# Attention and two expert layers on one core: another order of the steps up to the third block of the first experts

## The chip, the cores and the metric

The kernel runs on one core of a Trainium2 chip. The metric is the device time of one execution in microseconds (us); lower is better. The engines are called by the profile's names: PE is TensorE (PEld its weight loads), DVE is VectorE, ACT is ScalarE, POOL is GpSimd, SP is the engine whose queue issues every DMA of this kernel.

## The reference

A gated linear attention over 768 time steps (2 batches, 8 heads of 40) is followed by two expert layers on 1536 tokens of width 320. All inputs are 64-bit floats.

```python
m_new = np.maximum(f_gate[:, :, t] + m, i_gate[:, :, t])
f_stab = np.exp(f_gate[:, :, t] + m - m_new)
i_stab = np.exp(i_gate[:, :, t] - m_new)
C = f_stab * C + i_stab * np.einsum('bhd,bhe->bhde', vt, kt)
n = f_stab * n + i_stab * kt
y[:, :, t] = sigmoid(o_gate) * (C @ qt) / np.maximum(np.abs(n . qt), 1.0)
...
x = (x @ w_a) * (x @ w_b) @ w_out          # first experts, 320 -> 1536 -> 320
h = x @ w_in                               # second experts, 320 -> 2048 -> 320
x = np.maximum(0.01 * h, h) @ w_out
```

## The kernel before

The time axis is cut into six pieces `p` of 128 steps, for each of the two batches `b`. A piece of attention goes through these steps (the names are those in the table `ORDER`, the lines those of the profile): `dsc` (L351) scans the forget gates into a 128x128 decay for four heads on DVE; `smm` (L373) forms the scores on PE; `sat` (L378) multiplies both on DVE; `out` (L422) forms the outputs on PE; `onm` (L433 to L435), `og` (L440, POOL), `nrm` (L481) and `nd` (L486, ACT) divide by the norm and apply the output gate; `xmm` (L493) transposes the result, and `xh` (L507, ACT) and `xl` (L513, DVE) split it into a rounded part and a rest. `stm` (L448) and `ste` (L468) form the state that the next piece starts from; `gist` (L323, L324) transposes the input gates.

Ahead of the first piece stand the gates: `lg` loads them (the first 128 steps as `lg:0`, the other 640 as `lg:1`), `gs` (L274) scans them, `gfa`, `gfb`, `gi` (L281, L285, L289) take differences, `gef` and `gei` (L292) take exponentials on ACT, `gfr` (L295 to L297) rounds the first 128, `gdec` (L300, L301) and `gcum` (L309) prepare the other pieces, `dmm` (L341) spreads the first piece's gates over the partitions, and `idr` (L699) copies four identities for the scans.

The weights arrive as 64-bit floats in tiles of 128 x 768 (or 640) words. `lw` (L209) loads one: 128 x 768 x 8 bytes are 0.786 MB. `dh` (L224) and `dl` (L228) decode its two halves on ACT, `dm` (L232) joins them on DVE, `dr` (L241, L251) rounds on ACT, `ds` (L246, L247, L256) forms the rest on POOL. `up` (L562) multiplies a block of tokens with one pair of weight tiles: it takes four passes over `xh` first, then passes over `xl`, for each of two halves. The blocks 0 and 1 of the first experts have 256 tokens (one piece of both batches), the third, block 2, has 512. `e1`, `em`, `eh`, `el` work on the product, and `dn` (L620 to L622) multiplies it with the second weight matrix.

`spin` (L329) is a matmul over a tile of zeros, 512 columns wide, into a PSUM tile that nobody reads.

The order is written out by hand: `ORDER` lists all 1116 steps, and the last loop of the kernel issues them one after the other. So each engine works off its own instructions in the order of the table, and waits at an instruction until what that one needs is there. A load on SP also waits for the load eight places ahead of it, and for the buffer that it fills.

Of the kernel before, what the change touches and what calls it, by code (L numbers as in the profile page):

```python
# [37 lines left out]
    dm:2 onm:0:1 dm:4 out:0:0 lc:1 lf:1:0 lw:3 scum dr:4 og:0:1 smm:1:0 dsc:1:0:1 onm:0:0 dh:3 dr:2 dsc:1:0:0
    og:0:0 lw:6 lk:1:0 lq:1:0 ld:1:0 stm:0:0 stm:0:1 ds:4 sat:1:0:0 nrm:0:1 nrm:0:0 lf:1:1 sat:1:0:1 dl:3
    ste:0:1 nd:0:0 ds:2 val:1:0 ste:0:0 nd:0:1 vo:1:0 xmm:0:0 xmm:0:1 xh:0:0 lk:1:1 lw:5 ls:1:1 lw:7 lq:1:1  # L40
    ld:1:1 xh:0:1 xl:0:0 xl:0:1 up:0:1 up:0:0 dm:3 dl:6 dh:6 qry:1:0 dr:3 e1:0:1 e1:0:0 dm:6 em:0:1 em:0:0
    sig:1:0 eh:0:0 eh:0:1 out:1:0 ds:3 el:0:1 onm:1:0 el:0:0 dsc:1:1:1 up:0:3 dr:6 dh:5 sig:1:1 dl:5 val:1:1
    og:1:0 ds:6 vo:1:1 qry:1:1 dm:5 up:0:2 lw:8 e1:0:3 nrm:1:0 em:0:3 dsc:1:1:0 e1:0:2 dn:0:0 smm:1:1 dh:7 dl:7
    dr:5 nd:1:0 sat:1:1:0 sat:1:1:1 em:0:2 dm:7 lk:2:0 lq:2:0 lw:9 eh:0:2 up:0:4 lf:2:0 dl:8 dr:7 eh:0:3 out:1:1
    xmm:1:0 dh:8 key:1:0 ds:5 onm:1:1 dn:0:1 el:0:2 el:0:3 dn:0:2 og:1:1 xh:1:0 e1:0:4 nrm:1:1 xl:1:0 em:0:4
    dm:8 ds:7 dn:0:3 nd:1:1 stm:1:0 xmm:1:1 eh:0:4 dl:9 xh:1:1 up:0:5 dr:8 xl:1:1 ste:1:0 ds:8 e1:0:5 up:1:0
    em:0:5 el:0:4 lw:10 ls:2:0 lk:2:1 vo:2:1 val:2:0 key:1:1 up:1:1 smm:2:0 dh:9 eh:0:5 e1:1:0 dsc:2:0:0 dm:9
    em:1:0 el:0:5 dh:10 dl:10 eh:1:0 e1:1:1 dr:9 sat:2:0:0 dsc:2:0:1 sat:2:0:1 el:1:0 em:1:1 lq:2:1 lw:12 lw:11
    ld:2:0 ls:2:1 stk:1:0 key:2:0 dn:0:4 up:1:3 dn:0:5 stm:1:1 dn:1:0 eh:1:1 e1:1:3 dl:12 el:1:1 dm:10 em:1:3
    dn:1:1 up:1:2 up:1:4 dr:10 dh:11 eh:1:3 e1:1:2 em:1:2 vo:2:0 ds:9 qry:2:0 ds:10 el:1:3 sig:2:1 e1:1:4 eh:1:2  # L50
    stm:2:0 up:1:5 ste:1:1 em:1:4 el:1:2 dh:12 eh:1:4 e1:1:5 up:0:6 lf:2:1 lw:13 lf:3:0 ld:2:1 ls:3:0 lw:15
    dm:12 el:1:4 dl:11 e1:0:6 dsc:2:1:0 em:1:5 ls:4:0 em:0:6 lk:3:1 dsc:2:1:1 dm:11 dn:1:2 dn:1:3 up:0:7 dn:1:4
    out:2:0 eh:1:5 dh:13 dr:11 eh:0:6 dr:12 sig:2:0 el:1:5 dsc:3:0:1 e1:0:7 up:1:6 onm:2:0 em:0:7 key:2:1
    ste:2:0 el:0:6 e1:1:6 eh:0:7 dl:13 ds:12 ds:11 val:2:1 og:2:0 up:1:7 dn:0:6 dn:1:5 el:0:7 em:1:6 nrm:2:0
    dm:13 smm:2:1 qry:2:1 stk:1:1 lw:14 lw:16 lf:3:1 up:0:8 dl:15 e1:1:7 eh:1:6 dr:13 sat:2:1:0 dl:14 dh:14
    el:1:6 stk:2:0 ds:13 dl:16 nd:2:0 em:1:7 sat:2:1:1 eh:1:7 dh:15 e1:0:8 dsc:3:1:0 dn:1:6 out:2:1 dn:0:7
    up:0:9 em:0:8 el:1:7 dm:14 dn:1:7 dm:15 stm:2:1 onm:2:1 dsc:3:1:1 dr:14 up:1:8 e1:0:9 eh:0:8 dr:15 og:2:1
    val:3:1 ds:14 em:0:9 ste:2:1 nrm:2:1 nd:2:1 dh:16 eh:0:9 el:0:8 e1:1:8 xmm:2:1 xmm:2:0 up:1:9 dn:0:8 el:0:9
    ld:3:1 lk:3:0 lw:17 em:1:8 ds:15 vo:3:0 lq:3:0 ls:3:1 lk:4:0 lf:4:0 lq:3:1 dm:16 eh:1:8 e1:1:9 xh:2:0 xh:2:1
    xl:2:0 em:1:9 dsc:3:0:0 eh:1:9 ld:3:0 dr:16 sig:3:0 xl:2:1 stk:2:1 ds:16 vo:3:1 el:1:8 dn:0:9 up:0:10  # L60
    up:1:10 val:4:0 val:3:0 qry:3:0 dn:1:8 smm:3:0 e1:0:10 dl:17 sig:3:1 dh:17 el:1:9 em:0:10 e1:1:10 eh:0:10
    sat:3:0:0 el:0:10 sat:3:0:1 dm:17 dr:17 dn:1:9 up:0:11 key:3:1 em:1:10 out:3:0 eh:1:10 e1:0:11 el:1:10
    onm:3:0 em:0:11 up:1:11 eh:0:11 e1:1:11 og:3:0 ds:17 key:3:0 vo:4:0 qry:3:1 nrm:3:0 smm:3:1 el:0:11 dn:0:10
    sat:3:1:0 em:1:11 dn:0:11 stm:3:0 sat:3:1:1 eh:1:11 nd:3:0 out:3:1 ste:3:0 el:1:11 onm:3:1 xmm:3:0 dn:1:10
    dn:1:11 lq:4:0 xh:3:0 ls:5:1 og:3:1 nrm:3:1 xl:3:0 nd:3:1 xmm:3:1 stk:3:0 xh:3:1 ye:0 xl:3:1 stm:3:1 up:2:0
    dsc:4:0:0 ste:3:1 e1:2:0 em:2:0 lk:5:1 ld:4:0 smm:4:0 dsc:4:0:1 key:4:0 qry:4:0 up:2:1 sat:4:0:1 sat:4:0:0
    eh:2:0 e1:2:1 ye:1 lf:5:1 ls:4:1 lf:4:1 ld:4:1 lk:4:1 stm:4:0 out:4:0 em:2:1 el:2:0 dsc:4:1:1 eh:2:1 sig:4:0
    onm:4:0 dsc:5:1:0 lq:4:1 dn:2:0 up:2:2 e1:2:2 el:2:1 em:2:2 vo:5:1 og:4:0 up:2:3 dn:2:1 eh:2:2 sig:4:1
    e1:2:3 ste:4:0 nrm:4:0 el:2:2 em:2:3 dsc:4:1:0 lk:5:0 lf:5:0 lq:5:0 ld:5:0 ls:5:0 smm:4:1 dn:2:2 up:2:4
    eh:2:3 e1:2:4 sat:4:1:1 sig:5:1 em:2:4 el:2:3 up:2:5 stk:3:1 val:5:0 qry:5:0 key:4:1 val:4:1 val:5:1 qry:4:1  # L70
    eh:2:4 e1:2:5 sat:4:1:0 dsc:5:0:1 em:2:5 el:2:4 vo:4:1 nd:4:0 stk:4:0 up:2:6 xmm:4:0 dn:2:3 out:4:1 dn:2:4
    eh:2:5 e1:2:6 em:2:6 el:2:5 xh:4:0 eh:2:6 up:2:7 e1:2:7 el:2:6 onm:4:1 og:4:1 dsc:5:0:0 nrm:4:1 nd:4:1
    xl:4:0 em:2:7 stm:4:1 xmm:4:1 up:2:8 eh:2:7 sig:5:0 xh:4:1 e1:2:8 dn:2:5 dsc:5:1:1 em:2:8 el:2:7 ste:4:1
    xl:4:1 lq:5:1 ld:5:1 up:2:9 smm:5:0 e1:2:9 eh:2:8 sat:5:0:1 em:2:9 sat:5:0:0 el:2:8 up:2:10 smm:5:1 dn:2:6
    qry:5:1 stk:4:1 vo:5:0 sat:5:1:0 sat:5:1:1 e1:2:10 eh:2:9 out:5:1 dn:2:7 out:5:0 em:2:10 onm:5:0 onm:5:1
    og:5:0 og:5:1 up:2:11 el:2:9 nrm:5:0 nrm:5:1 e1:2:11 nd:5:1 nd:5:0 xmm:5:1 xmm:5:0 xh:5:0 eh:2:10 xh:5:1
    dn:2:8 em:2:11 el:2:10 xl:5:0 xl:5:1 ca lw:19 lw:20 dn:2:9 up:4:0 e1:4:0 dh:19 eh:2:11 lw:21 em:4:0 el:2:11
    up:4:1 dn:2:10 dn:2:11 dh:20 eh:4:0 dl:19 dl:20 e1:4:1 dm:20 el:4:0 em:4:1 dm:19 eh:4:1 dr:19 up:4:2 e1:4:2
    dh:21 dr:20 ye:2 dl:21 ds:19 ds:20 lw:25 lw:18 em:4:2 el:4:1 up:4:3 dn:4:0 ym:0:1 ym:0:0 eh:4:2 lw:22 yh:0:1
    yh:0:0 e1:4:3 em:4:3 yl:0:0 el:4:2 dn:4:1 dm:21 up:4:4 dh:22 dl:22 dr:21 e1:4:4 eh:4:3 dl:18 dh:25 dh:18  # L80
    yl:0:1 ym:0:2 em:4:4 el:4:3 dn:4:2 ds:21 up:4:5 yh:0:2 dl:25 e1:4:5 eh:4:4 em:4:5 lw:26 dm:18 dm:25 el:4:4
    dn:4:3 ym:0:3 up:4:6 dm:22 dh:26 dr:25 eh:4:5 dr:22 dl:26 e1:4:6 yl:0:2 dm:26 el:4:5 em:4:6 dn:4:4 dr:18
# [721 lines left out]
```

## Time and profile before

| | before |
|---|---|
| time, median of 3 runs | 449.29 us (448.03 to 450.08) |
| the profiled execution's own time | 449.11 us |
| its span, first to last instruction | 447.3 us |
| PE busy | 434.6 us (97%) |
| DVE, ACT, POOL busy | 210.6, 208.6, 126.3 us |
| HBM read | 44.1 MB |

The span is cut into 40 slices on the profile's page, and one digit gives the busy tenths of a slice. Waits are listed with the engine and line that waited and what ended the wait. The timeline lists instructions by start, with the idle time of the engine ahead of them in square brackets. The granted clock of TensorE is 1.00 at 2.4 GHz and 0.50 at 1.2 GHz.

### The profile page before, as it was taken

How to read it: one execution, taken by the hardware profiler on the slowest of the kernel's cores; microseconds unless marked ns; L12 is line 12 of the kernel's file. 1: busy time of each engine (PE TensorE's matmuls, PEld its weight loads, DVE VectorE, ACT ScalarE, POOL GpSimd, SP SyncE). 2: the span in 40 equal slices, each digit the busy share in tenths (PEclk: the TensorE clock that was granted, in tenths of full speed). 3: DMA queues.
4: the chain of work that ended last, by engine and by line, in shares of the span. 5: the costliest groups of instructions: out<-in, count | busy, mean ns of one | idle time of the engine just before them, and what ended most of it. 6: DMA issues, size and time to landing. Idle time of an engine off the chain costs nothing.

```text
span 447.3 us, 8216 instructions
## 1 busy us (share of the span) xinstructions
PE 434.6 (97%) x3350; PEld 391.2 (87%) x3350; DVE 210.6 (47%) x352; ACT 208.6 (47%) x381; POOL 126.3 (28%) x135
## 2 busy tenths in 40 slices
PE   6789999999999999999999999999999999999996
...
PEclk9559999999999999999999999999999999999999
...
GB/s 247 292 320 284 301 235 268 231 211 55 141 170 94 61 34 1 1 186 106 134 59 139 110 171 77 8 52 0 1 59 1 1 1 1 1 59 1 0 1 59
DMA packets 25799, 46.69 MB, mean 104 GB/s; under 512 B 1885, under 2 KB 18849, under 8 KB 25761
## 3 DMA queue, kind: packets, MB, share of 16 engines
...
q8 instruction: 26, 0.43, 0.4%
q14 instruction: 12, 0.10, 0.1%
...
## 4 chain that ended last, share of the span: by engine, by line
PE 91%; DVE 4%; ACT 1%; issue 1%; POOL 1%; DMA 1%; SPq 0%; DVEq 0%; ACTq 0%
PE mm L562 29%; PE mm L589 20%; PE dn L620 11%; PE dn L622 11%; PE dn L621 11%; PE pa L373 2%; PE pa L422 1%; DVE pp L351 1%; PE pa L415 1%; PE pa L493 1%; PE pa L448 1%; DVE y L232 1%; PE pa L652 1%; DMA ident_all<-consts 1%; PE mm L448 1%
## 5 line engine op out<-in xcount | busy, mean ns | idle before, releaser
L562 PE MATMUL mm<-xh,wa 128*128 128x256 f32 (+1 forms) x480 | 116.4, 343 | 0.6 <-ACT xh L507 0.6
L562 PEld LDWEIGHTS mm<-xh,wa 128*128 128x128 f32 x480 | 80.9, 192 | 10.2 <-ACT xh L507 1.0
L605 DVE TENSOR_TENSOR gl<-gg,gh 128x512 fp32r<-128x512 f32 x48 | 34.2, 730 | 99.4 <-ACT gh L600 95.3
L562 PE MATMUL mm<-xl,wa 128*128 128x256 f32 (+1 forms) x288 | 79.9, 339 | 0.0
L595 ACT ACTIVATE gg<-mm 128x512 f32<-128x512 f32 x48 | 28.1, 595 | 72.3 <-PE mm L589 70.9
L620 PE MATMUL dn<-wa,gh 128*128 128x320 f32 x192 | 59.5, 310 | 0.0
L622 PE MATMUL dn<-wa,gl 128*128 128x320 f32 x192 | 59.3, 309 | 0.0
L621 PE MATMUL dn<-wa,gh 128*128 128x320 f32 x192 | 59.2, 309 | 0.0
L562 PEld LDWEIGHTS mm<-xl,wa 128*128 128x128 f32 x288 | 51.9, 192 | 5.8
L572 DVE TENSOR_TENSOR gg<-gg,mm 128x256 f32<-128x256 f32 (+1 forms) x48 | 26.2, 546 | 59.4 <-PE mm L562 35.3
L567 ACT ACTIVATE gg<-mm 128x256 f32<-128x256 f32 (+1 forms) x48 | 23.4, 488 | 61.9 <-PE mm L562 43.8
L620 PE MATMUL dn<-wd,gh 128*128 128x320 f32 x144 | 46.0, 319 | 0.0
L622 PE MATMUL dn<-wd,gl 128*128 128x320 f32 x144 | 44.6, 310 | 0.4 <-DVE gl L581 0.4
L621 PE MATMUL dn<-wd,gh 128*128 128x320 f32 x144 | 44.4, 308 | 0.0
L581 DVE TENSOR_TENSOR gl<-gg,gh 128x256 fp32r<-128x256 f32 (+1 forms) x48 | 36.8, 770 | 11.4 <-ACT gh L576 11.3
L600 ACT ACTIVATE gh<-gg 128x512 fp32r<-128x512 f32 x48 | 29.8, 630 | 21.7 <-PE dn L621 21.3
L576 ACT ACTIVATE gh<-gg 128x256 fp32r<-128x256 f32 (+1 forms) x48 | 25.0, 523 | 30.9 <-DVE gg L572 23.9
L621 PEld LDWEIGHTS dn<-wa,gh 128*128 128x128 f32 x192 | 36.0, 188 | 1.3
L620 PEld LDWEIGHTS dn<-wa,gh 128*128 128x128 f32 x192 | 36.0, 188 | 1.2
L622 PEld LDWEIGHTS dn<-wa,gl 128*128 128x128 f32 x192 | 36.0, 188 | 0.0
L589 PE MATMUL mm<-yh,wa 128*128 128x512 f32 x120 | 35.8, 395 | 0.0
L589 PE MATMUL mm<-yh,w 128*128 128x512 f32 x120 | 35.6, 394 | 0.0
...
## 6 DMA issues: line engine op xcount, KB each, us to landing
...
```

Of the source, the lines that this page charges most:

```text
L562: pe.matmul(halves_[ab], w[:, slot, ab, :], xs[lo][:, kt, cs], start=i == 0, stop=i == 7)
L567: act.activation(out=g, in_=up_t[blk, f][0], func=AF.Copy)
L572: dve.tensor_tensor(out=g, in0=g, in1=up_t.pop((blk, f))[1], op=ALU.mult)
L576: act.activation(out=gh, in_=g_t[blk, f], func=AF.Copy)
L581: dve.tensor_tensor(out=gl, in0=g_t.pop((blk, f)), in1=raw_view(gh_t[1, blk, f]), op=ALU.subtract)
L589: pe.matmul(ps, w[:, slot, f % 2, :], xs[lo][:, kt, :], start=i == 0, stop=i == 7)
L595: act.activation(out=g, in_=ps, func=AF.Prelu, alpha=0.01)
L600: act.activation(out=gh, in_=g_t[2, blk, f], func=AF.Copy)
L605: dve.tensor_tensor(out=gl, in0=g_t.pop((2, blk, f)), in1=raw_view(gh_t[2, blk, f]), op=ALU.subtract)
L620: pe.matmul(ps, gh[:, cs], w[:, 0, :], start=f == 0, stop=False)
L621: pe.matmul(ps, gh[:, cs], w[:, 1, :], start=False, stop=False)
L622: pe.matmul(ps, gl[:, cs], w[:, 0, :], start=False, stop=f == last)
```

## The change

The first 560 of the 1116 steps stand in another order; the steps are the same ones, with the same arguments, and the other 556 are untouched. The reordered stretch goes from the gates to the fourth of the twelve weight pairs of block 2. The head of the table, whose rows show the places that matter here:

```diff
-    lg:0 init spin spin spin spin spin spin spin spin spin spin spin spin spin spin spin spin lg:1 lw:1 lc:0
-    ls:0:1 gs:0 lw:0 lk:0:1 ls:0:0 lw:2 gfa:0 gs:1 gfa:1 sel gfb:0 gfb:1 gi:0 smm:0:1 gi:1 dh:1 idr gef:1 gef:0
...
+    lg:0 init spin spin lw:1 spin spin spin dh:1 dl:1 lg:1 lc:0 lw:0 gs:0 gfa:0 gs:1 dh:0 gi:0 gfb:0 gef:0 gfa:1
+    lw:2 dm:1 sel dl:0 gfb:1 dm:0 ls:0:1 gfr gef:1 lk:0:1 gei:0 gdec gcum spin gi:1 dmm:1:1 ls:0:0 sdec dr:0 dr:1
...
```

Line numbers of the kernel after are three lower than those of the kernel before, since the table is three lines shorter.

On ACT, at the start of the program, the rows before (`y` is a raw weight tile, `wd` holds the gates, `fr` the first gates rounded, `wa` a rounded weight tile; a DMA number in brackets is the load that is waited for):

```order
L224 ACTIVATE y<-y 128x768 [waits DMAHW2_49]
L699 ACTIVATE idr<-ident_all 128x512 [waits DMAHW3_49]
L292 ACTIVATE wd<-wd 16x640 [waits DVE_49]
L292 ACTIVATE wd<-wd 64x128
L228 ACTIVATE y<-y 128x768
L295 ACTIVATE fr<-wd 64x128 [waits Activation_49]
L292 ACTIVATE wd<-wd 16x128 [waits DMAHW0_49,DVE_49]
L292 ACTIVATE wd<-wd 16x640 [waits DMAHW1_49,DVE_49]
L300 ACTIVATE wd<-wd 16x640
L241 ACTIVATE wa<-y 128x768 [waits DVE_49]
```

and at the same place after:

```order
L221 ACTIVATE y<-y 128x768 [waits DMAHW1_49]
L225 ACTIVATE y<-y 128x768
L221 ACTIVATE y<-y 128x768 [waits DMAHW4_49]
L289 ACTIVATE wd<-wd 64x128 [waits DVE_49]
L225 ACTIVATE y<-y 128x768
L292 ACTIVATE fr<-wd 64x128 [waits Activation_49]
L289 ACTIVATE wd<-wd 16x640 [waits DVE_49]
L289 ACTIVATE wd<-wd 16x128 [waits DMAHW0_49]
L297 ACTIVATE wd<-wd 16x640 [waits Activation_49]
L238 ACTIVATE wa<-y 128x768 [waits DVE_49]
L238 ACTIVATE wa<-y 128x768
L696 ACTIVATE idr<-ident_all 128x512 [waits DMAHW3_49]
```

The decode of the second weight tile (`dh:0`, third row after, which waits for the load `lw:0`) and its other half (`dl:0`, fifth row) now stand ahead of the first gates' exponential and rounding, and both roundings and `idr` behind them; `idr` was the second row before.

On PE, in the middle of the first piece of attention, the rows before:

```order
L341 MATMUL pa<-fr,sel 128x128 x3
L323 MATMUL mm<-ident_all,wd 128x16 [waits DMAHW1_49,Activation_49]
L323 MATMUL mm<-ident_all,wd 128x16 x4
L373 MATMUL dn<-stk 128x128 [waits DMAHW0_49]
L373 MATMUL dn<-stk 128x128 [waits DMAHW1_49]
L373 MATMUL dn<-stk 128x128 x6
L422 MATMUL dn<-kvo,at 32x41 [waits DMAHW7_49,DVE_49,Pool_49]
```

and after:

```order
L338 MATMUL pa<-fr,sel 128x128 x3
L326 LDWEIGHTS gg
L326 MATMUL dn<-gg 128x512
L419 MATMUL dn<-kvo,at 32x41 [waits DMAHW0_49,DVE_49,Pool_49]
L419 MATMUL dn<-kvo,at 32x41 x15
L419 MATMUL dn<-kvo,at 32x41 [waits DVE_49]
L419 MATMUL dn<-kvo,at 32x41 x15
L326 LDWEIGHTS gg
L326 MATMUL dn<-gg 128x512
L370 MATMUL dn<-stk 128x128 [waits DMAHW1_49,PE_49]
```

Of the sixteen spins six stay at the start, and ten stand singly, in a pair or as three between the attention's matmuls up to the first `up`; the transposes of `gist` moved behind the scores of the next piece.

## Rows read from the trace of the kernel before

**Rows 1.** The page's slices: PE busy, and the clock granted to TensorE.

```profile
PE   6789999999999999999999999999999999999996
PEclk9559999999999999999999999999999999999999
```

**Rows 2.** Waits of PE over the whole program: us, times, longest.

```profile
PE mm L562 <- ACT xh L507: 0.6, 1, 0.6
...
PE dn L622 <- DVE gl L581: 0.4, 1, 0.4
```

**Rows 3.** Stretches: width, busy PE, PEld, DVE, ACT, POOL; clock, DMA share, GB/s.

```profile
0.00:5.00 5.00, 4.00 (x12) 1.52 (x13) 1.45 (x5) 1.28 (x1) 0.41 (x5) 1.00 0.42 127
5.00:10.00 5.00, 2.67 (x22) 1.55 (x19) 4.36 (x8) 2.90 (x5) 1.54 (x1) 1.00 0.97 329
10.00:11.00 1.00, 0.29 (x2) 0.13 (x1) 1.00 (x4) 1.00 (x4) 0.45 (x1) 0.91 1.02 409
15.00:20.00 5.00, 4.69 (x88) 3.98 (x87) 5.00 (x8) 2.42 (x3) 4.03 (x7) 0.50 1.04 330
31.25:34.65 3.40, 3.40 (x16) 3.40 (x17) 2.79 (x3) 2.55 (x3) 3.40 (x4) 0.50 1.06 380
```

**Rows 4.** Timeline of the gates up to the first scan: start, us, engine, line.

```profile
1.48 0.63 SPq L680 DMA_DIRECT2D wd<-gates  x1
2.15 0.58 SPq L209 DMA_DIRECT2D y<-w  x1
...
5.98 1.54 POOL L281 TENSOR_TENSOR wd<-wd 16x640 f32<-16x640 f32 x1 [5.04 <-DVE wd L274]
6.36 0.90 ACT L224 ACTIVATE y<-y 128x768 f32<-128x768 f32 x1 [4.34 <-DMA y<-w]
6.54 1.01 DVE L694 TENSOR_TENSOR sel<-ident_all 64x16 fp32r<-64x16 f32 x1 [0.64 <-DMA ident_all<-consts]
...
11.17 1.11 PE L341 MATMUL mm<-fr,sel 64*128 64x128 f32 x4 [0.24 <-POOL fr L297]
...
13.18 1.22 DVE L351 TENSOR_TENSOR_SCAN pp<-pa,idr 128x512 f32<-128x512 f32 x1 [1.00 <-PE pa L341]
```

**Rows 5.** Groups by form from 0 to 36 us: count, busy us, mean ns.

```profile
L224 ACT ACTIVATE y<-y 128x768 f32<-128x768 f32 x5 | 4.6, 912 | 7.5 <-DMA y<-w 7.5
...
L378 DVE TENSOR_TENSOR at<-dn,pp 128x512 f32<-128x512 f32 x4 | 2.7, 685 | 0.1
...
L292 ACT ACTIVATE wd<-wd 16x640 f32<-16x640 f32 x2 | 1.5, 728 | 0.7 <-DVE wd L285 0.7
...
L699 ACT ACTIVATE idr<-ident_all 128x512 f32<-128x512 f32 x1 | 0.6, 612 | 0.0
...
L292 ACT ACTIVATE wd<-wd 64x128 f32<-64x128 f32 x1 | 0.3, 292 | 0.0
```

**Rows 6.** Timeline of DVE, POOL and PE in the first piece and the first up.

```profile
3.53 0.15 PEld L329 LDWEIGHTS <-gg 128*128 128x128 bf16 x1 [0.28 <-issue]
3.96 1.63 PEld L329 LDWEIGHTS <-gg 128*128 128x128 bf16 x8 [0.28 <-issue]
...
22.77 2.21 PE L373 MATMUL pa<-stk 40*128 40x128 f32 x16
23.93 0.72 POOL L440 TENSOR_TENSOR kvo<-kvo,rec 128x320 f32<-128x320 f32 x1 [2.24 <-ACT kvo L402]
24.62 1.23 DVE L351 TENSOR_TENSOR_SCAN pp<-pp,idr 128x512 f32<-128x512 f32 x1 [0.90 <-DMA pp<-fdr]
24.91 2.60 PE L448 MATMUL mm<-kvo 128*120 128x123 f32 x12
29.53 1.02 DVE L468 TENSOR_TENSOR ct<-mm,mask 120x246 f32<-120x246 f32 x4
30.59 1.20 DVE L513 TENSOR_TENSOR xl<-pa,xh 128x384 fp32r<-128x384 f32 x2
31.25 1.22 PE L562 MATMUL mm<-xh,wa 128*128 128x256 f32 x4 [0.58 <-ACT xh L507]
```

More of the change, by code (lines that the diff above doesn't have):

```diff
@@ L38 @@
[L38 to L82, printed above, removed]
@@ new lines @@
+    lw:2 dm:1 sel dl:0 gfb:1 dm:0 ls:0:1 gfr gef:1 lk:0:1 gei:0 gdec gcum spin gi:1 dmm:1:1 ls:0:0 sdec dr:0 dr:1
+    dmm:1:0 dmm:0:0 idr lw:4 ds:1 dsc:0:1:1 gist:0 dl:2 val:0:1 lf:1:0 gei:1 vo:0:1 dsc:0:1:0 key:0:1 dh:2 smm:0:1
+    lk:0:0 dh:4 dmm:0:1 dm:2 ds:0 sat:0:1:0 sat:0:1:1 dsc:0:0:0 spin ls:1:0 vo:0:0 sig:0:1 lw:3 dl:4 lc:1 dsc:0:0:1
+    out:0:1 val:0:0 dsc:1:0:0 spin dm:4 key:0:0 smm:0:0 scum spin dr:4 sat:0:0:0 dr:2 lw:6 dsc:1:0:1 spin onm:0:1
+    stm:0:1 smm:1:0 sig:0:0 sat:0:0:1 lq:1:0 gist:1 sat:1:0:0 ld:1:0 dh:3 spin og:0:1 nrm:0:1 lk:1:0 out:0:0 ds:2
@@ new lines @@
+    nd:0:1 lf:1:1 xmm:0:1 spin onm:0:0 og:0:0 nrm:0:0 spin ds:4 lw:5 xh:0:1 sat:1:0:1 xl:0:1 lw:7 spin dl:3 ste:0:1
+    nd:0:0 xmm:0:0 ls:1:1 spin xh:0:0 dm:3 xl:0:0 stm:0:0 dl:6 dh:6 qry:1:0 ld:1:1 ste:0:0 sig:1:0 dr:3 val:1:0
+    vo:1:0 ds:3 dm:6 spin dr:6 up:0:1 dsc:1:1:0 e1:0:1 lq:1:1 lk:1:1 dh:5 out:1:0 up:0:0 dl:5 onm:1:0 og:1:0 em:0:1
+    eh:0:1 e1:0:0 dm:5 dh:7 up:0:3 em:0:0 ds:6 eh:0:0 el:0:1 qry:1:1 nrm:1:0 val:1:1 up:0:2 el:0:0 dl:7 e1:0:3
+    e1:0:2 nd:1:0 dsc:1:1:1 dm:7 smm:1:1 vo:1:1 dr:7 sat:1:1:1 dn:0:0 dn:0:1 xmm:1:0 dr:5 lw:9 sat:1:1:0 out:1:1
@@ new lines @@
+    key:1:0 lw:8 em:0:3 ds:5 em:0:2 sig:1:1 eh:0:2 up:0:4 xh:1:0 onm:1:1 og:1:1 eh:0:3 el:0:2 xl:1:0 lf:2:0 ds:7
+    nrm:1:1 e1:0:4 dl:9 el:0:3 em:0:4 dn:0:2 dl:8 eh:0:4 stm:1:0 dsc:2:0:0 dn:0:3 el:0:4 nd:1:1 xmm:1:1 up:0:5
+    xh:1:1 dh:8 lk:2:0 xl:1:1 val:2:0 ste:1:0 e1:0:5 up:1:0 key:1:1 ls:2:0 smm:2:0 e1:1:0 em:1:0 lw:10 dm:8 sig:2:0
+    up:1:1 stk:1:0 eh:1:0 dr:8 sat:2:0:0 em:0:5 el:1:0 stm:1:1 dn:1:0 ds:8 e1:1:1 em:1:1 dn:0:4 dsc:2:0:1 dh:9
+    lq:2:0 lw:12 eh:1:1 up:1:3 lk:2:1 dh:10 dm:9 sat:2:0:1 dl:10 ste:1:1 dl:12 el:1:1 up:1:2 dr:9 lw:11 e1:1:3
```

84 lines of the change are left out of this document (56 added, 28 removed).

## The prediction

> **What bounds the kernel now.** I read the slices first. PE is at 9 tenths from the fourth slice to the end [rows 1], so from about 35 us on the time is PE's own work. The list of PE's waits then says how complete that is: the last waits are 0.6 us for `xh` ahead of the first `up` and 0.4 us in one `dn` later [rows 2]; behind the first `up` nothing else is waited for. What can move the time is therefore where the dense work begins, at which clock, and whether a new wait appears inside it.
>
> The first `up` starts at 31.25 us [rows 6]. The clock falls during the slice 10 to 11 us and is at 0.50, the lower of its two levels (1.2 of 2.4 GHz), still from 31.25 to 34.65 [rows 3]. In these 3.4 us PE did what takes 1.7 at full clock. So I count the dense work as beginning, at full clock, at 31.25 + 1.7 = 32.95 us; this is the number to compare.
>
> What holds the first `up` back is a chain on DVE. It starts with the first scan at 13.18 [rows 4] and ends with the second `xl` at 30.59 + 1.20 = 31.79 [rows 6], 18.6 us in which DVE waited 0.9 (for `pp`) [rows 6]; from 15 to 20 it was busy 5.00 of 5 us while PE ran at half clock [rows 3]. Ahead of it stands the gates' chain over ACT and POOL to the spreading matmuls at 11.17 [rows 4].
>
> **The change, part by part.** *The gates' chain.* On ACT, `dh:0` stands ahead of the first gates' exponential, so that waits for the load `lw:0`. In the new order of loads, what is ahead of the end of `lw:0` is 0.066 MB (`lg:0`), two weight tiles of 0.786, `lg:1` 0.082 and the identity 0.066, by the shapes in the code 1.79 MB. Before, 127 GB/s over the first 5 us moved 0.635 MB, and then 329 GB/s [rows 3], which gives 5 + 1.15/0.329 = 8.5 us. The first weight tile is issued 0.67 us sooner (1.48 instead of 2.15, [rows 4]): 7.85. Before, the first tile was complete by the same count at 5.9 and was waited for until 6.36 [rows 4], so 0.45 comes on top: 8.3 us, between 7.9 (no lag) and 8.8 (none of the earlier issue gained).
>
> From there ACT works through, with the means of [rows 5]: `dh:0` 0.91, `gef:0` 0.29, `dl:0` (the other half of the same tile, taken like the first) 0.91, `gfr` 0.29, `gef:1` 0.73, `gei:0` 0.29 (both by the small form), `gdec` 0.73 (by the large form), `dr:0` and `dr:1` (the same 128 x 768, taken like the decode) 0.91 each, `idr` 0.61: 6.6 us, to 14.9. In this row `gef:1` may have to wait for DVE, up to 0.5 us, so I take 15.2, between 14.5 and 15.9. The first scan needs `idr`, and it is the last of the row; before, `idr` was ready long ahead and the scan came at 13.18. The matmuls at 11.17 move too, to about 11, and hide behind it. **Term 1: the DVE chain starts 2.0 us later** (1.3 to 2.7).
>
> Beside the 0.5: `sel`, 16 columns wide, took 1.01 us from 6.54 to 7.55, and POOL's difference ran from 5.98 to 7.52 [rows 4]. So a DVE operation can be held as long as POOL's lasts; after, `gi:0`, `gfb:0` and `dm:1` stand where that POOL operation runs.
> The Trainium skill, SBUF — State Buffer, section "SBUF: two separate sides", says that DVE and GpSimd share one pair of ports under an exclusive lock for an operation with two SBUF inputs; the end at 7.55 against 7.52 agrees. By it the first scan would stand at 15.4 to 15.9, and without it at 14.9.
>
> *The DVE chain itself.* From the first scan to the `xl` that the first `up` needs last, the same steps stand in it: six scans, six `sat`, three `dm`, two `onm`, two `nrm`, two `xl`. One pair of `ste` of the two (1.02 us for four instructions, [rows 6]) now stands behind: -0.5. The 0.9 us wait for `pp` goes, since that load is issued ahead of two others and the scan that needs it comes 2 us later. So 18.6 - 0.9 - 0.5 = 17.2 us of work. New is that the second `onm`, its `og` and its `nrm` stand next to each other: `nrm` waits for `og` on POOL, 0.7 us [rows 6]. That gives an end at 15.2 + 17.2 + 0.7 = 33.1 us if PE delivers in time.
>
> *PE between the pieces.* It doesn't, if its clock is low. DVE has its second `sat` done about 4.55 us into the chain, at 19.75: two scans of 1.2 [rows 4], a copy, a `dm` of about 0.8, two `sat` of 0.69 [rows 5], each a little overlapped with the next. At half clock PE then has half of `out` (0.65, `out` taken as 1.3 like half of the twelve `stm` matmuls), a spin (0.43, from 3.53 to 3.96, the distance of two spins' loads), `smm` 2.2, two spins 0.85, `stm` 1.3, `smm` 2.2 [rows 6] and `gist` (about 0.7), 8.35 us, to 28.1, when DVE, with four more scans, a `dm`, two `sat` and an `onm`, has come to `gist`'s copy at about 26.95: 1.15 us of waiting. Then a spin and `out` end at 29.85, with DVE there at 29.25: 0.6 more. At full clock PE needs half and DVE waits for neither. **Term 2: the last `xl` at 34.85 us at the low clock, 33.1 at the high one.** The ten spins that now stand in the row cost up to 0.43 us each; four are in this sum, one stands ahead of it, and five fill the time between `out` and the first `up`, where PE would wait for DVE.
>
> *The start of the dense work.* An `up` runs four passes over `xh` before it needs `xl`, 0.5 us at full clock, so it may begin that much ahead. The spins, transposes and the last `stm` make PE's row unbroken from about 28 us on, where before it stood 0.6 us right ahead of `up` [rows 2]. So I take it that the clock is up when `up` begins: full-clock start 34.85 - 0.5 = 34.35, against 32.95. **Sum: +1.4 us.**
>
> *Inside the dense work.* POOL and DVE are both later by about what PE is, and the weights of the next `up` steps are ready 3 us or more ahead by the same counting, so I add nothing. PE waited once for 0.4 us there before [rows 2], so at most 0.4 can be gained; what can be lost is bounded by the same kind of wait at several places, 0 to 2 us.
>
> The profiled execution took 449.11 us for a span of 447.3; the same 1.8 stand around it. 449.11 + 1.4 = 450.5. The median, 449.29, is 0.04% above that execution, which changes nothing.
>
> **The rivals.** *A: the clock rises early.* If it is up by 25 us, PE holds nobody up, the last `xl` is at 33.1, the full-clock start 32.6: -0.35 us, 448.8. For it: PE is busy without a gap from about 18 us on, with full-width spins in between. Against it: from 15 to 20 us before, PE was busy 4.69 of 5 us and the clock stayed at 0.50 throughout [rows 3].
> The Trainium skill, TensorE: Matmul & The Clock Gate, section "Part 1: The HAM clock gate", says that the low clock is the default and that sustained activity releases it; by that alone this rival would be the forecast, 448.8. The stretch from 15 to 20 us speaks against taking mere busy time for activity.
>
> *B: the clock rises late, and the kernel is slower.* If the mixed row of spins and small matmuls doesn't bring the clock up, the first `up` follows the last spin at about 35 us at half clock, and loses again the 1.7 us that it lost before: 34.85 - 0.25 + 1.7 = 36.3 against 32.95, +3.3 us, 452.4. It decides at the first `up`: clock 0.50 there, and this holds. For it: the same stretch from 15 to 20 us; against it: at the start a row of spins alone went from 0.43 us each (3.53 to 3.96) to 0.2 each (eight in 1.63) [rows 6], so spins do count.
>
> *C: a new wait in the dense work.* 2 us on top of the forecast, 452.5. For it: DVE is nearly full up to 60 us and every `em` there frees a PSUM buffer for an `up`; against it, the counts above show some us in hand.
>
> *D: the start comes early after all.* The new loads bring `lw:0` sooner than the bytes say and the chain over DVE is shorter in a way that I don't see: 2.5 us or more gained, 446.6. Against it: even with 7.9 us for `lw:0` the first scan can't come before 14.5.
>
> **How the numbers follow.** A measurement of this kernel can tell about 0.5% from no change, 2.25 us. Forecast 450.5: 0.42. A, 448.8: 0.20. B, 452.4: 0.22. C: 0.10. D: 0.06. The forecast and A are within 0.5% (447.04 to 451.54); B and C beyond it; of the forecast's own spread (term 1 by 0.7 either way) a little passes the bound, and a little of B and C, with an early `lw:0`, stays below it. Faster 0.06, same 0.62, slower 0.32. The range goes from A with an early load, 448.2, to B with a late one, 453.2; D and the worst of C are left out.
>
> **What would show it.** The first scan at 15 to 16 us, waiting for ACT's `idr`, shows term 1; at 13 it would be wrong, and with it the sum. DVE waiting for PE at the copy of `gist` and at `onm` shows term 2. The clock at the first `up` tells the forecast from A and B: 0.50 from 10 us until some point between 28 and 35 in the forecast. The first `up` should start at 34 to 35 us. PE waits behind it of more than 1 us would be C.

## The result, and the profile after

| | before | after |
|---|---|---|
| time, median of 19 runs each | 448.9 us (448.03 to 450.08) | 452.46 us (449.2 to 454.14) |
| ratio after/before, 95% interval | | 1.0069 (1.0055 to 1.0084) |
| the profiled execution's own time | 449.11 us | 449.38 us |
| its span | 447.3 us | 447.6 us |
| PE busy | 434.6 us | 430.0 us |

The change makes the kernel 0.7% slower, and it makes its time uncertain: before, the runs lie within 2 us, after, within 5. The profiled execution of after is one of the quickest and is only 0.3 us longer than that of before. So the first trace alone can't show where 3.5 us went; a trace of a longer execution, of 453.29 us, comes with the experiments (e9). Two executions of the experiments, one of e1 (853.09 us) and one of e4 (479.96 us), ran far slower than all others of their kernels and are left out of the medians, ranges and ratios.

The page's slices of after, PE busy and granted clock; they answer to [rows 1]:

```profile
PE   2779999999999999999999999999999999999996
PEclk9999999999999999999999999999999999999999
```

Two things must be read with care. PE is idle for most of the first slice, since only six spins are left there. And the clock row says full speed from the start, although the matmuls don't run at it. The record reads 1.00 until its first entry, so the pace has to be taken from the matmuls themselves.

The timeline of after from the gates to the first scan (start, us, engine, line, in brackets the idle time ahead); it answers to [rows 4]:

```profile
3.11 0.42 DVE L271 TENSOR_TENSOR_SCAN wd<-wd 64x128 f32<-64x128 f32 x1 [2.17 <-DMA wd<-gates]
6.63 0.88 ACT L221 ACTIVATE y<-y 128x768 f32<-128x768 f32 x1 [4.61 <-DMA y<-w]
8.56 2.61 POOL L278 TENSOR_TENSOR wd<-wd 16x640 f32<-16x640 f32 x1 [7.63 <-DVE wd L271]
9.66 1.53 DVE L691 TENSOR_TENSOR sel<-ident_all 64x16 fp32r<-64x16 f32 x1
9.77 0.89 ACT L221 ACTIVATE y<-y 128x768 f32<-128x768 f32 x1 [1.47 <-DMA y<-w]
13.40 1.11 PE L338 MATMUL mm<-fr,sel 64*128 64x128 f32 x4 [9.67 <-POOL fr L294]
15.37 0.61 ACT L696 ACTIVATE idr<-ident_all 128x512 f32<-128x512 f32 x1
16.02 1.22 DVE L348 TENSOR_TENSOR_SCAN pp<-mm,idr 128x512 f32<-128x512 f32 x1 [0.56 <-ACT idr L696]
```

The first scan starts at 16.02 us instead of 13.18, and it waits for ACT's `idr`, the end of the row that begins with the decode at 9.77. That is the prediction's first term.

The timeline of after from there to the first `up`; it answers to [rows 6]:

```profile
16.36 2.08 PE L370 MATMUL dn<-stk 40*128 40x128 f32 x16
24.83 1.16 PE L370 MATMUL pa<-stk 40*128 40x128 f32 x16
29.98 0.49 DVE L478 TENSOR_TENSOR ya<-dn,kvo 128x320 f32<-128x320 f32 x1 [0.90 <-POOL kvo L437]
31.21 0.52 PE L490 MATMUL pa<-ident_all,ya 128*128 128x128 f32 x3 [1.32 <-DVE at L375]
32.38 0.82 PE L559 MATMUL mm<-xh,wa 128*128 128x256 f32 x4
32.88 0.55 DVE L510 TENSOR_TENSOR xl<-pa,xh 128x384 fp32r<-128x384 f32 x1
33.48 0.51 PE L559 MATMUL mm<-xl,wa 128*128 128x256 f32 x2 [0.28 <-DVE xl L510]
```

The sixteen score matmuls tell the clock: 2.08 us at 16.36 (before, at 0.50, they took 2.21 [rows 6]) and 1.16 us at 24.83. Sixteen more between them, at 21.93, took 1.87. So in this execution the clock came up between 21.9 and 24.8 us and was up at the first `up`. That `up` starts at 32.38 and waits 0.28 us for the second `xl`; its passes over `xl` start at 33.48, as they would behind an undisturbed full-clock start at 33.0, against 32.95 of before. The spans differ by 0.3 us, 447.6 against 447.3.

### The profile page after: what moved, and what is told of

Read it like the earlier page. It is cut to its first block, busy times and chain, and to the rows that moved or that the text cites. A ratio compares the mean times of both kernels' runs of the same rounds, so it can differ in the third digit from the quotient of the medians.

```text
span 447.6 us, 8211 instructions
## 1 busy us (share of the span) xinstructions
PE 430.0 (96%) x3350; PEld 386.8 (86%) x3350; DVE 210.9 (47%) x352; ACT 208.7 (47%) x381; POOL 130.8 (29%) x135
## 4 chain that ended last, share of the span: by engine, by line
PE 87%; DMA 5%; POOL 3%; DVE 2%; issue 1%; ACT 1%; SPq 0%; POOLq 0%; ACTq 0%
PE mm L559 27%; PE mm L586 20%; PE dn L617 11%; PE dn L619 11%; PE dn L618 11%; DMA y<-w 2%; PE pa L370 2%; PE pa L419 2%; PE pa L412 1%; DMA kvo<-kvo 1%; DMA wd<-gates 1%; PE pa L445 1%; PE pa L649 1%; DMA fdr<-wd 1%; PE pa L490 1%
## 5 line engine op out<-in xcount | busy, mean ns | idle before, releaser
L559 PEld LDWEIGHTS mm<-xh,wa 128*128 128x128 f32 x480 | 79.8, 189 | 9.3
L569 DVE TENSOR_TENSOR gg<-gg,mm 128x256 f32<-128x256 f32 (+1 forms) x48 | 26.1, 545 | 50.7 <-PE mm L559 24.8
L573 ACT ACTIVATE gh<-gg 128x256 fp32r<-128x256 f32 (+1 forms) x48 | 24.8, 523 | 32.7 <-DVE gg L569 27.5
```

What stands on the lines that cost most here:

```text
L559: pe.matmul(halves_[ab], w[:, slot, ab, :], xs[lo][:, kt, cs], start=i == 0, stop=i == 7)
L569: dve.tensor_tensor(out=g, in0=g, in1=up_t.pop((blk, f))[1], op=ALU.mult)
L573: act.activation(out=gh, in_=g_t[blk, f], func=AF.Copy)
```

## The experiments

The kernel before and the changed kernel are called so; "at the front" means behind `init`. Where a kernel's table takes another number of lines, its line numbers shift by two or so. A mean granted clock c of an execution is turned into time at the low clock by 2 x (1 - c) x span; this counts only what stands behind the record's first entry. The first trace of after, slow at 16.36 us, has a mean clock of 0.999, so a mean near 1 doesn't tell when the clock came up. The medians:

| run | what it is | median, us (range) | ratio to before, 95% |
|---|---|---|---|
| e1 | after, all 16 spins at the front | 451.86 (449.42 to 452.73) | 1.0052 (1.0035 to 1.0070) |
| e2 | before, 10 of its 16 spins spread | 448.12 (447.58 to 449.23) | 0.9977 (0.9965 to 0.9989) |
| e3 | after, 40 more spins at the front | 450.59 (449.87 to 452.16) | 1.0040 (1.0024 to 1.0056) |
| e4 | after, gates loaded first | 450.82 (448.27 to 453.32) | 1.0030 (1.0008 to 1.0051) |
| e5 | after again | 453.43 (450.51 to 454.45) | 1.0088 (1.0061 to 1.0114) |
| e6 | e4 with ACT's row of before | 451.44 (450.21 to 452.36) | 1.0052 (1.0033 to 1.0072) |
| e7 | before, 17 more spins spread | 448.86 (446.79 to 450.16) | 0.9991 (0.9977 to 1.0005) |
| e8 | e3 with 15 more spins in the gaps | 451.29 (450.44 to 452.42) | 1.0053 (1.0036 to 1.0071) |
| e9, e10 | after, one execution each | 453.29 and 449.71 | |
| e11 | after, one decode later | 453.23 (450.86 to 455.12) | 1.0091 (1.0065 to 1.0116) |
| e12 | e11 with 10 more spins at the front | 451.49 (449.74 to 452.6) | 1.0049 (1.0030 to 1.0067) |

### e1: the spins back at the front

```diff
-    lg:0 init spin spin lw:1 spin spin spin dh:1 ...
+    lg:0 init spin spin spin ... (16 of them) lw:1 dh:1 ...
```

The other eleven spins of the changed kernel are taken out: ten from between the attention's matmuls, and one that follows the front's five on PE with no matmul between.

> The kernel after, with all 16 spins at the front and none among the attention's matmuls. Theory (the new order starts the scans 2.8 us later, and only the spins in between bring the clock up before the dense work): first scan at 16.0 as in the kernel after, clock low until the first up or later, first up at 34 to 35 us, 452.5 to 454 us in nearly every run. Rival (the spins in between cost PE time and are what makes the kernel after slower): 449 to 450 us.

The median, 451.86, is 0.6 us below after's, and the intervals of the two ratios overlap; the theory's 452.5 to 454 and the rival's 449 to 450 both missed it. So neither a help nor a cost of the ten spins inside the attention is shown. By mean clock the executions were at the low clock for 24 to 28 us. The only trace is of the execution of 853.09 us, so where the others began their first `up` isn't known.

### e2: the spins of before spread out

```diff
-    lg:0 init spin spin spin ... (16 of them) lg:1 lw:1 lc:0
+    lg:0 init spin spin spin spin spin spin lg:1 lw:1 lc:0
...
-    xmm:0:0 xmm:0:1
+    spin spin spin spin xmm:0:0 xmm:0:1
...
-    up:0:1 up:0:0
+    spin spin up:0:1 up:0:0
```

Four more stand singly ahead of `out:0:1`, `out:0:0`, `smm:1:0` and `stm:0:0`.

> The kernel before, with six spins at the front and ten among the attention's matmuls, the order otherwise untouched. Theory (spins in between are covered by DVE's chain and can only bring the clock up sooner): first scan at 13.2, first up at 31.0 to 31.8 us, 447.3 us in runs where the clock rises before the first up, 449 where it rises behind it, none above 449.5. Rival (the spins in between cost time of their own): 450 to 451 us.

The timeline of e2 shows a clock that came up and fell again:

```profile
23.37 1.16 PE L368 MATMUL pa<-stk 40*128 40x128 f32 x16
28.82 1.05 PE L488 MATMUL pa<-ident_all,ya 128*128 128x128 f32 x6 [1.94 <-DVE ya L476]
30.46 1.23 PE L557 MATMUL mm<-xh,wa 128*128 128x256 f32 x4
```

The scores at 23.37 run at full clock; PE then stands for 1.94 us, and the first `up` at 30.46 takes 1.23 us for four passes, the half pace of [rows 6]. It still starts 0.8 us sooner than in before. The nine executions lie where the theory put them (none above 449.5), and this is the only kernel of the study that is quicker than before clear of noise, by 0.23%.

### e3 and e8: enough spins to keep the clock up

e3 is after with 40 spins more at the front; e8 adds to it ten ahead of `dmm:0:1` and five ahead of `xmm:0:0`.

```diff
-    lg:0 init spin spin lw:1
+    lg:0 init spin spin spin ... (40 more) spin spin lw:1
...
+    spin spin spin spin spin spin spin spin spin spin
     dmm:0:1
...
+    spin spin spin spin spin
     xmm:0:0
```

> The kernel after with 40 more spins at the front, where PE has nothing to do until 13.4 us. Theory (the order's later scans cost nothing more once the clock is up early; the median of the kernel after is made by runs in which it rises late): clock up from 4 us through the dense work, last xl at 33.1 to 33.5 us, 449.0 to 449.6 us in every run, a spread below 1 us. Rival (the order costs its 3 us at full clock too): 452 us or more.

> The changed kernel with 40 more spins at its front, as in the run before, and 10 more ahead of the last spreading matmuls and 5 ahead of the last transposes, to fill the 2.4 us for which PE waited there before the clock fell. Theory (the clock decides, and at full clock the new order costs 0.5 us at most): the clock stays up from 13 to 35 us, the first up starts at 33 to 33.6 at full clock, and the time is 448.9 to 449.8 us with a spread under 1 us. Rival (the new order itself costs the time, by the late first scan or by the spins as work): 451 us or more with the clock up.

Both missed, since the clock didn't stay up. The timelines of e3 (three rows of PE, two of DVE) and of e8 (one row of PE):

```profile
15.36 1.16 PE L370 MATMUL dn<-stk 40*128 40x128 f32 x16
18.91 1.08 PE L338 MATMUL pa<-fr,sel 64*128 64x128 f32 x4 [2.38 <-DVE pp L348]
22.25 2.08 PE L370 MATMUL dn<-stk 40*128 40x128 f32 x16
29.08 0.24 DVE L321 COPY istn<-mm 128x80 f32<-128x80 f32 x1 [1.32 <-PE mm L320]
30.90 0.17 DVE L430 TENSOR_SCALAR den<-dn 128x8 f32<-128x8 f32 x1 [0.58 <-PE dn L419]
```

```profile
24.97 2.64 PE L370 MATMUL pa<-stk 40*128 40x128 f32 x16 [1.60 <-DMA stk<-stk]
```

In e3 the clock is up by 15.36 us, PE waits 2.38 us for a scan, and the same sixteen matmuls then take 2.08 us again. In e8 that gap is filled, and the next one, 1.60 us for a load, does the same: the sixteen matmuls behind it take 2.64 us. At full clock PE is so quick that it has to wait for DVE or a load, and each of these two waits was followed by the low clock.

At the low clock, e3 shows the prediction's second term: DVE waits 1.32 us at the copy of `gist` (1.15 foretold) and 0.58 us at `onm` (0.6 foretold). The first `up` stood at 34.81 us.

### e4 and e6: the gates' chain

e4 loads the second gates and the identity ahead of the first weight tile. e6 does so too, and puts ACT's row back: `idr` first, the decode behind the gates' exponentials, the join `dm:0` behind the first scan, `dr:0` behind that.

```diff
-    lg:0 init spin spin lw:1 spin spin spin dh:1 dl:1 lg:1 lc:0 lw:0
+    lg:0 init spin spin lg:1 lc:0 lw:1 spin spin spin dh:1 dl:1 lw:0
```

```diff
-    dh:1 ... dh:0 ... dl:0 ... dm:0 ... gdec ... dr:0 dr:1 ... idr ... dsc:0:1:1
+    idr dh:1 ... gdec dh:0 dl:0 ... dr:1 ... dsc:0:1:1 dm:0 dr:0
```

> The kernel after with lg:1 and the identity loaded ahead of the first weight tile, as in the kernel before; the order on every engine but SP is that of the kernel after. Theory of the prediction (ACT's row from lw:0 to idr sets the first scan): the second gate scan starts at 4.4 us instead of 6.9, but the first decay scan still at 15.7 to 16.4, time within 0.5 us of the kernel after, 452 to 453. Rival (the late lg:1 shifts all of DVE's work): first decay scan at 13.5 to 14.5 us, 2 us less than the kernel after, 450 to 450.5.

> The changed kernel with the gates loaded ahead of the second weight tile (as in the run before), and with ACT's row of before: the identities first, the decode of the second weight tile behind the gates' exponentials, its join on DVE behind the first scan. Theory (ACT's row from the decode to the identities sets the first scan): the first scan moves from 15.25 to between 13.4 and 14.6 us, where DVE's own row or PE's spreading matmuls set it, and the time is 0.5 to 1.5 us below that run's 450.84 median, 449.3 to 450.3. Rival (something else holds the scan): it stays at 15.0 to 15.5 and the time at 450.5 to 451.2.

The first scan in e4, and in e6 with what came next on DVE and PE:

```profile
15.25 1.22 DVE L346 TENSOR_TENSOR_SCAN pp<-mm,idr 128x512 f32<-128x512 f32 x1 [0.49 <-ACT idr L694]
```

```profile
13.95 1.20 DVE L346 TENSOR_TENSOR_SCAN pp<-mm,idr 128x512 f32<-128x512 f32 x1
18.93 1.25 DVE L227 SCALAR_TENSOR_TENSOR y<-y 128x640 int32<-128x640 int32 x1 [1.71 <-ACT y L219]
20.10 1.27 DVE L373 TENSOR_TENSOR at<-dn,pp 128x512 f32<-128x512 f32 x2
20.88 1.33 PE L417 MATMUL dn<-kvo,at 128*32 128x41 f32 x64 [1.89 <-POOL wa L241]
33.82 0.55 DVE L508 TENSOR_TENSOR xl<-pa,xh 128x384 fp32r<-128x384 f32 x1
```

Second gates 2.6 us earlier in e4 move the scan by only 0.8: ACT's row sets it. The time of e4 fell by more, to 450.82 where 452 to 453 was expected and the rival had 450 to 450.5; with no trace of after near its own median, why isn't shown. With that row undone the scan is at 13.95 with no wait ahead, where the theory put it. But the time didn't follow (451.44 against 449.3 to 450.3 expected). ACT, with the moved decode behind the exponentials, now comes late to the next tile; the join of that tile on DVE waits 1.71 us for it, ahead of the first two `sat`, and PE waits 1.89 us for the first `out` (the row names POOL, whose operation ended at the same time as the first `sat`). The second `xl` is at 33.82, later than in after's first trace. So in this trace what comes off ACT's row ahead of the scan comes back behind it; the scan is 2.07 us earlier than in after's first trace (16.02), and the median shows no gain over e4.

### e7: more spins in the kernel before

```diff
+    spin spin spin spin spin spin spin spin spin spin
     xmm:0:0 xmm:0:1
...
+    spin spin spin
     up:0:1 up:0:0
```

and one each ahead of four other steps, as in e2, with the 16 at the front kept.

> The kernel before with its 16 spins kept at the front and 17 more put into the first piece of attention: one each at four places, 10 ahead of the last transposes and 3 ahead of the first up. Theory (what costs time before is the half clock at the first up, 1.7 us): the row of spins in front of the transposes keeps the clock up, the first up starts at full clock and the time is 446.6 to 447.6 us, 1.3 to 2.3 below before, in executions where the clock rose in time; where it didn't, the ten spins at 0.43 us each fill a wait of about 1 us and cost the rest, up to 450. Rival (a spin is only work, the clock doesn't follow it): 450.5 or more throughout.

The trace is of 449.6 us:

```profile
25.86 2.46 PE L444 MATMUL mm<-kvo 128*120 128x123 f32 x12
28.11 3.46 PE L325 MATMUL dn<-gg 128*128 128x512 bf16 x10
32.86 0.73 PE L558 MATMUL mm<-xh,wa 128*128 128x256 f32 x4
```

The clock was still low when the ten spins began; they took 3.46 us where PE had about 1 us to fill, but the first `up` runs at full clock (0.73 us for four passes). Both branches of the expectation occurred: the two quickest of twelve runs took 446.79 and 447.46 us, the rest 448.0 to 450.16. The quick branch has no trace.

### e5, e9 and e10: the changed kernel again

No edit: the question is what the longer executions of it do.

> The changed kernel itself, unaltered, to see more executions of it and a second trace. The profiled execution of it took 449.38 us with the clock up from about 22.5 us on, and is one of the quickest; the median was 452.46. Theory (the executions differ only in when the clock rises): the times spread again from 449 to 454 us, median 451.5 to 453; if this trace is one above 452, its first up starts at 34.8 to 35.5 us at half clock (clock 0.50 over 30 to 35 us) and nothing behind the first up waits more than in the first trace. Rival (the longer executions lose their time inside the dense work): such a trace has its first up at 33 to 34 us, and PE waits of 2 us or more behind it.

> The changed kernel itself, for a third trace of it. Both traces so far are from its quicker executions (449.38 and 450.51 us). Theory (late or low clock at the first up): if this execution takes over 452 us, the first up starts at 34.5 to 35.5 us at a granted clock of 0.50, or the clock falls in PE's wait of 1.3 us ahead of the second transpose, at about 31 us, and is back some 3 us behind the first up; no other wait is longer by over 0.5 us than in the first trace. Rival (another wait): the clock is 1.00 at the first up, which starts at 33 to 34 us, and 2 us are lost behind it in waits that the first trace doesn't have.

> The changed kernel itself, for a fourth trace of it, with the same expectation: over 452 us goes with the lower clock at the first up (a start at 34.5 to 35.5 us at 0.50, or a fall at about 31 us); below 451 us with a first up at 33 to 34 us at full clock. Rival: a difference of 2 us with the same start and clock, lost in waits behind the first up.

e5's trace (450.51 us) and e10's (449.71) have the clock up at the first `up`, like the first one; e9's is of a longer execution, 453.29 us. The second row of scores ahead of the first `up`, which took 1.16 us at 24.83 in the first trace; one row each from e5, e9 and e10, in this order:

```profile
26.58 1.22 PE L368 MATMUL pa<-stk 40*128 40x128 f32 x16
26.09 1.41 PE L368 MATMUL pa<-stk 40*128 40x128 f32 x16
24.79 1.22 PE L368 MATMUL pa<-stk 40*128 40x128 f32 x16
```

They run at or near full pace; the scores ahead of them, at about 22 us, still took 2.08, 2.08 and 1.67. So the clock came up at 26 to 27 us in e5 and e9, where the first `up` starts at 33.29 and 33.00, and at 22 to 24 in the first trace and e10, where it starts at 32.38 and 32.46.

PE's row of e9, then ACT and DVE at the same place, and the clock behind it (stretch, width, busy PE, PEld, DVE, ACT, POOL, clock, DMA share, GB/s):

```profile
33.00 0.82 PE L557 MATMUL mm<-xh,wa 128*128 128x256 f32 x4
40.90 0.28 PE L557 MATMUL mm<-xl,wa 128*128 128x256 f32 x1
43.20 1.22 PE L557 MATMUL mm<-xh,wa 128*128 128x256 f32 x4 [2.02 <-DVE gg L567]
47.85 0.41 PE L615 MATMUL dn<-wd,gh 128*128 128x320 f32 x1
```

```profile
39.81 0.80 ACT L219 ACTIVATE y<-y 128x640 f32<-128x640 f32 x1 [2.55 <-DMA y<-wd]
41.31 1.50 DVE L227 SCALAR_TENSOR_TENSOR y<-y 128x640 int32<-128x640 int32 x1 [2.39 <-ACT y L223]
42.73 0.41 DVE L567 TENSOR_TENSOR gg<-gg,mm 128x256 f32<-128x256 f32 x1
```

```profile
43.00:44.00 1.00, 0.80 (x3) 0.81 (x4) 0.95 (x4) 1.00 (x3) 0.00 (x0) 0.55 0.82 230
44.00:45.00 1.00, 1.00 (x6) 1.00 (x6) 1.00 (x2) 0.98 (x2) 0.00 (x0) 0.50 1.01 358
45.00:46.00 1.00, 1.00 (x7) 1.00 (x6) 1.00 (x2) 0.00 (x0) 0.21 (x1) 0.50 1.03 397
46.00:47.00 1.00, 1.00 (x9) 0.87 (x10) 0.33 (x1) 0.13 (x1) 1.00 (x1) 0.74 0.97 398
```

The same place in the first trace of after:

```profile
36.56 0.78 ACT L221 ACTIVATE y<-y 128x640 f32<-128x640 f32 x1
39.11 0.42 DVE L569 TENSOR_TENSOR gg<-gg,mm 128x256 f32<-128x256 f32 x1
43.52 0.41 PE L617 MATMUL dn<-wd,gh 128*128 128x320 f32 x1
```

Read it from the load. `lw:5`, the second tile of the `dn` weights, isn't complete until 39.81 us (in the first trace it was there by 36.56). ACT takes its decode `dh:5` in order and stands for 2.55 us; the join `dm:5` on DVE waits for ACT; behind the join stands the product `em:0:0` (L567), which frees the PSUM buffer that the fourth `up` writes. So PE stands for 2.02 us, for a weight that it needs only some steps later. Then the clock is low for 3.4 us of records and takes another 0.45 + 0.50 + 0.50 + 0.26 = 1.7. Start of the first `up` 0.62 later, wait 2.02, clock 1.7: 4.3 us, which is what the first `dn` shows (47.85 against 43.52); 3.9 of them reach the end (span 451.5 against 447.6).

So neither half of the expectation was whole: the clock is up at the first `up`, at 33.0 us (the rival), and a fall of the clock costs as much as the wait (the theory, at another place). In e5 and e10 ACT's decode waited for the same load (e5's row first):

```profile
38.97 0.80 ACT L219 ACTIVATE y<-y 128x640 f32<-128x640 f32 x1 [1.46 <-DMA y<-wd]
38.28 0.80 ACT L219 ACTIVATE y<-y 128x640 f32<-128x640 f32 x1 [1.61 <-DMA y<-wd]
```

There PE waited 0.4 us at this product. In these three traces the load comes about 8 us behind its issue (e9 31.95 to 39.81; e5 31.1 to 38.97; e10 30.3 to 38.28), so when it comes hangs on when SP gets to it; in the first trace it was issued at 30.10 and there within 6.5 us.

Over all 27 executions of the changed kernel (19, e5's six, e9, e10): twelve have a mean clock of 0.998 or more and take 449.2 to 453.6 us, six of them up to 450.51 and six from 451.01 on; five have 0.992 to 0.996, e9 among them, and take 453.25 to 454.45; two have 0.973 to 0.977 (451.53 and 452.46); eight have 0.965 or 0.966, 31 us at the low clock, and take 453.25 to 454.36. None of the last eight has a trace, nor has any of the six from 451.01 on.

### e11 and e12: the decode out of the way, and the front filled

```diff
-    lk:1:1 dh:5 out:1:0 up:0:0 dl:5 onm:1:0 og:1:0 em:0:1 eh:0:1 e1:0:0 dm:5 dh:7 up:0:3 em:0:0
+    lk:1:1 out:1:0 up:0:0 onm:1:0 og:1:0 em:0:1 eh:0:1 e1:0:0 dh:7 up:0:3 em:0:0
...
-    up:0:2 el:0:0 dl:7 e1:0:3 e1:0:2 nd:1:0 dsc:1:1:1 dm:7
+    up:0:2 dh:5 el:0:0 dl:5 dl:7 e1:0:3 e1:0:2 nd:1:0 dsc:1:1:1 dm:5 dm:7
```

e12 is e11 with ten more spins at the front.

> The changed kernel with one weight tile's decode (dh:5, dl:5, dm:5) moved behind the copies and products of the first two up steps, so that ACT and DVE no longer wait for that load ahead of them. In the trace of 453.29 us the load was complete at 39.8 us, the product that frees a PSUM buffer waited behind the join, PE stood still for 2.0 us at 41 us and then ran 3.5 us at half clock; in the trace of 449.38 us the load was there at 36.5 and PE didn't wait. Theory (this wait, not only the clock at the first up, makes the executions above 451 us): PE's wait for the product L567 is gone, and the median falls from 452.5 to 453.4 us to between 449.8 and 451.8. Rival (the long executions are long by the clock at the first up alone): the median stays at 452 to 453.5.

> The run before it with 10 more spins at the front, so that 16 stand there as in the kernel before. In the kernel before, and in the run with all spins at the front, the clock came up by 5 us, fell at 10 us and stayed at 0.50 until 35 us. Theory (a late clock at the first up costs the new order about 3 us, as the prediction's rival B): most executions are low for 24 to 32 us, the first up starts at 34 to 35.5 us at 0.50, and the time is 452 to 453.8. Rival (the interleaved spins bring the clock up by 25 us whatever stands at the front): the time is as in the run before it, below 451, with under 20 us at the low clock.

e11's trace, of 451.89 us, on ACT, DVE and PE:

```profile
42.02 0.91 ACT L221 ACTIVATE y<-y 128x768 f32<-128x768 f32 x1 [2.79 <-DMA y<-w]
44.73 2.49 DVE L229 SCALAR_TENSOR_TENSOR y<-y 128x640 int32<-128x640 int32 x2
47.88 0.55 PE L490 MATMUL pa<-ident_all,ya 128*128 128x128 f32 x3 [1.56 <-DVE at L375]
```

PE's wait for the product is gone, as foretold. But the moved decode `dh:5` now stands on ACT behind `dh:7`, the decode of another tile, for whose load `lw:7` ACT stands 2.79 us (the first row). So two joins stand together on DVE, 2.49 us, ahead of the next piece's `sat`, and PE waits 1.56 us for that instead. The median, 453.23, is where it was. The theory's time was missed; since the edit took one wait away and made another, the run doesn't tell what the first wait costs in the median.

e12 came out at 451.49, 1.7 us below e11 by the medians of six runs each; the intervals of the two ratios still overlap a little, and the two traces don't show the difference, since e12's is of its longest execution (452.6 us), has the same two joins, and PE waits 1.53 us behind them. The ten added spins lie in time that PE spends waiting anyway: with them PE still waits 6.1 us for the gates, where it waited 9.8. That they act through the clock is likely, but not shown. Theory B missed here: the clock wasn't late. By mean clock all six were low for 13 to 21 us, none for 31, and the trace has the clock at 0.50 from 10 us and up by 25. In e11 two of six were low for 31 us. What the expectation says of the clock of the run with all spins at the front (e1) is seen in no trace; only that run's mean clocks fit it.

## Why the prediction was right or wrong

**The range and the sign.** 452.46 lies in the range of 448.2 to 453.2 near its upper end. The likeliest single case was 450.5, within 0.5%; what came is slower by 0.69%, the outcome that had 0.32. The number is rival B's, 452.4, but B isn't what the one traced long execution shows. So its place in the range is in part luck: the forecast's own +1.4 us comes from term 2 at the low clock (without it the sum was -0.35), and in the four traces of after DVE waits at most 0.24 us at the copy of `gist` and not at all at `onm`.

**Term 1: right in kind, 0.8 us too small.** The first scan was foretold at 15.2 (14.5 to 15.9), waiting for `idr`; it waits for `idr` and stands at 16.02. The step that was mis-sized is the arrival of `lw:0`, 8.3 with a bound of 8.8, measured 9.77; a row 0.7 us shorter than summed hides part of these 1.5. The sum counted only the bytes ahead of it in the queue, 1.79 MB. The stretches of after, 0 to 5 and 5 to 10 us:

```profile
0.00:5.00 5.00, 2.74 (x6) 0.73 (x6) 0.81 (x4) 1.28 (x1) 0.41 (x5) 1.00 0.51 142
5.00:10.00 5.00, 0.00 (x0) 0.00 (x0) 3.06 (x5) 1.91 (x3) 1.44 (x1) 1.00 0.97 349
```

By 9.77 us 142 x 5 + 349 x 4.77 kB = 2.37 MB had moved, 0.6 MB more than stood ahead. So loads issued behind this one moved while it was still under way, which the sum had at nothing. ACT's row took 6.2 us (9.77 to 15.98) where 6.6 and up to 0.5 of waiting were summed; it waited 0.2.

The held operations were there: POOL's difference took 2.61 us instead of 1.54, and `sel` 1.53, ending together with it at 11.2 (in e4, with no POOL operation beside it, `sel` took 0.16). The Trainium skill, SBUF — State Buffer, section "SBUF: two separate sides", has DVE and GpSimd exclude each other on a shared pair of ports; the trace agrees, and this time POOL lost a us as well as `sel`.

**The DVE chain: right.** From the first scan to the end of the second `xl`, 16.02 to 33.43 is 17.4 us; 17.2 + 0.7 = 17.9 were foretold. The wait for `og` was 0.90 (0.7).

**Term 2: right at the low clock, which after's traces didn't have there.** e3 shows 1.32 and 0.58 us, e4 1.41 and 0.58, at the two places named, for 1.15 and 0.6.

**The clock: the first step that failed.** From [rows 3], a stretch of the kernel before, I took it that the clock rises between 28 and 35 us. In all four traces of after it rises between 22 and 27 us (rival A, which had 0.20 and 448.8; these executions took 449.4 to 450.5, or 453.3 with the wait); by mean clock eight of 27 executions were low for 31 us, which would be rival B's kind, though untraced. PE's row wasn't unbroken from 28 us on either: it waited 1.32 us at 31.21 in the first trace, with the clock up behind it. The row of small matmuls may not decide it alone: with ten more spins at the front, none of e12's six executions was low for 31 us, against two of e11's six. The Trainium skill, TensorE: Matmul & The Clock Gate, section "Part 1: The HAM clock gate", says that sustained activity releases the low clock; four traces of after agree, and the stretch from 10 to 31 us of before [rows 3] doesn't.

**"Inside the dense work I add nothing": the second step that failed.** The prediction said that the weights of the next `up` steps are ready 3 us or more ahead, and kept 0 to 2 us for rival C, with "every `em` there frees a PSUM buffer for an `up`" as its reason. The tile that mattered belongs to `dn`, whose decode stands ahead of those products on ACT and DVE; nothing was in hand for it: ACT waited for its load in three of four traces, 1.5 to 2.6 us. C's wait was 2.0 us in e9, at just that kind of place. Not foreseen was that the wait takes the clock down with it, so that C costs 3.7 instead of 2. C had a chance of 0.10; five of 27 executions have a mean clock that fits a short low stretch.

**What stays open.** That the five executions at 0.992 to 0.996 all are like e9 is argued from clock and time, with one trace; of the twelve at 0.998 or more, the longest (453.6) has none either. The eight at 0.965 aren't explained beyond their clock. Nor is the clock all of the spread: e8's six executions all have a mean clock of 0.992 and take 450.44 to 452.42 us. Two trials to take single causes away (e6, e11) moved the waits and not the median, so I can't give a share of the 3.5 us to each, and the cause of the median stays open. More spins at the front go with lower medians (e3 450.59 and e8 451.29 against after's 452.46 and e5's 453.43; e12 against e11), which points to the clock without proving it. The order itself, with the clock up at the first `up` and at most 0.4 us of waiting at that product, costs 0.3 to 1.4 us (449.38, 449.71 and 450.51 against 449.11, which has its first `up` at half clock).
